# Strassen blocks in the output projection of two batches, and v through DRAM from a later pair on, in a fused attention and bilinear FFN kernel

## The chip, the cores and the metric

The kernel runs on one core of one Trainium2 chip. The metric is device time in microseconds for one execution. A core has five instruction streams: PE (TensorE, matmuls), DVE (VectorE), ACT (ScalarE), POOL (GpSimd) and SP (SyncE, here only for issuing DMAs). SBUF is the memory in which tiles lie, and PSUM (`ps` in the profile, eight banks) takes what PE writes.

## The reference

```python
# q, k, v: (4 batches, 8 heads, 768 tokens, 64), float32; sort_net: (4, 8, 8, 8)
P = sort_net
for _ in range(5):                       # exp, then rows and columns normalised
    P = exp(P - max(P)); P = P / sum(P, -1); P = P / sum(P, -2)
k_sorted = einsum('bhij,bhjcd->bhicd', P, k_blocks)   # 8 blocks of 96 tokens are mixed
v_sorted = einsum('bhij,bhjcd->bhicd', P, v_blocks)
attn = softmax(q_blocks @ k_sorted.T / 8)             # within each block of 96
x = (attn @ v_sorted).transpose(...).reshape(3072, 512)
out = ((x @ w_a) * (x @ w_b)) @ w_out                 # 512 -> 1536 -> 512
```

## The kernel before, in words

The work runs batch by batch, and attention within a batch by pairs of heads (four pairs, named (batch, pair) below).

**Attention of a pair.** q, k and v come by POOL's DMA queue. PE transposes q (line 473) and mixes k with the block weights `s_all` (L489). v goes one of two ways, chosen by `VDMA(b, p)`. By PE: v is mixed as k is (L489), cast to `vT`, transposed on PE (L559) and copied to `vs`. Through DRAM: v is mixed the other way round by two matmuls (L537), cast to `vm`, stored to a DRAM tile `vd` by SP (L546) and read back by SP into `vs` in the order wanted (L550). Then come the scores (L578), the exponentials on ACT (L583), the products with v (L593), the normalisation on DVE (L599, L604), and the transposition into `xT`, for batch 1 and later by a transposing DMA on SP (L620). There is one `xT`, so a batch's `xT` can be written only when the batch before has been read out.

**First FFN layer.** For batch 0, plain matmuls (L749) give a and b in blocks of 128 by 384. For batches 1 to 3, `ab_strassen` (matmuls at L831) works by 2 by 2 blocks with seven products for eight. For each of six groups g it runs a chain for a and one for b. Its sums of weights (`ws_a`, `ws_b`) and of x (`tx`) are made ahead. ACT copies partial results out of a bank (`f<-ps`, L840), DVE adds another bank to them (`a<-f,ps`, `f<-f,ps`), and the product of a and b goes to `hT`. Three of the four products of a group read two SBUF tiles (`hT<-a,f`) and may run on POOL or on DVE; the fourth reads a bank (`hT<-a,ps`) and runs on DVE. All these DVE and POOL operations are issued by the helper `tt`, so they share one line, L306, and are told apart by their tiles.

**Output projection.** `out_plain` makes a chunk of 128 tokens by 512 columns with twelve matmuls of 512 columns (L899), six chunks a batch; ACT or DVE copies the bank to an `o` tile and SP stores it in two DMAs (L919).

**Order.** Every piece of work is an `Op` with its engines and their assumed durations, its predecessors, and the ring buffers and banks that it takes (`get`) and gives back (`put`). `Plan.solve` is a list scheduler: of all ready pieces it takes the one that can start first, with ranks for ties, and where a piece may run on several engines, the one that it takes to end first. What comes out is a fixed order of instructions for each engine; on the chip each engine runs its own in that order and waits on semaphores. The main loop gives the ranks: output projection of batch b, attention of batch b+2, then the first layer of batch b+1.

Of the kernel before, what the change touches and what calls it, by code (L numbers as in the profile page):

```python
# [9 lines left out]
FP32 = mybir.dt.float32  # L10
# [6 lines left out]
def _ap(t: bass.AP, extra_offset, pattern):  # L17
    return bass.AP(tensor=t.tensor, offset=t.offset + extra_offset,
                   ap=[list(p) for p in pattern])
# [16 lines left out]
class Plan:  # L36
# [12 lines left out]
    def add(self, eng, dur, fn, deps=(), get=(), put=(), rank=0.0, lat=None):  # L49
        alts = dict(eng) if isinstance(eng, (list, tuple)) else {eng: dur}  # L50
        op = Op(alts, fn, deps, list(get), list(put), rank, lat, len(self.ops))
        for key in op.put:
            self.holders[key] = self.holders.get(key, 0) + 1
        self.ops.append(op)
        return op
# [76 lines left out]
    def solve(self):  # L132
        self.banks, self.until = [0.0] * 7 + [self.warm_until], {}
        for op in self.ops:
            op.left = len(op.deps)
            for d in op.deps:
                d.users.append(op)
        at = dict(self.AT)
        ready = [op for op in self.ops if op.left == 0]
        done = 0  # L140
        while ready:
            cands = {}
            for op in ready:
                w = self._when(op)
                if w is None:
                    continue
                w = max(w, op.ready)
                ends = {e: max(at[e], w) + d for e, d in op.alts.items()}
                e = min(ends, key=ends.get)
                cands.setdefault(e, []).append((max(at[e], w), op))  # L150
            pick = None
            for e, c in cands.items():
                lo = min(s for s, _ in c) + self.EPS[e]
                s, op = min(((s, o) for s, o in c if s <= lo), key=lambda x: (x[1].rank, x[1].seq))
                if pick is None or (s, op.seq) < (pick[0], pick[2].seq):
                    pick = (s, e, op)
            if pick is None:
                raise RuntimeError("the plan is stuck: " + ", ".join(
                    f"{o.get}" for o in ready[:12]))
            s, e, op = pick  # L160
            ready.remove(op)
            op.start, op.eng, op.end = s, e, s + op.alts[e]
            at[e] = op.end
            self._take(op, s)
            lat = self.LAT[e] if op.lat is None else op.lat
            self._give(op, op.end + lat)
            for u in op.users:
                u.left -= 1
                u.ready = max(u.ready, op.end + lat)
                if u.left == 0:  # L170
                    ready.append(u)
            done += 1
        assert done == len(self.ops), f"{len(self.ops) - done} pieces of work wait for ever"
        self._fill()
        return sorted(self.ops, key=lambda o: (o.start, o.seq))
# [13 lines left out]
            t = max(t, o.end)  # L189


STRASSEN_AB = (1, 2, 3)
STRASSEN_OUT = ()
QDMA = lambda b, p: b >= 3
VDMA = lambda b, p: b >= 1


@with_exitstack
def kernel(
# [11 lines left out]
    nc = tc.nc  # L211
# [34 lines left out]
    def copy(eng, out, in_):  # L246
        if eng is nc.scalar:
            nc.scalar.copy(out=out, in_=in_)  # L248
        else:
            eng.tensor_copy(out=out, in_=in_)  # L250
# [3 lines left out]
    def ring(cls, n, shape, dtype):  # L254
        mats[cls] = [const.tile(shape, dtype, name=f"{cls}{i}") for i in range(n)]
        plan.slots(cls, n)
# [3 lines left out]
    def buf(key):  # L260
        cls, i = plan.where[key]
        if cls == "pair":
            touched.update((2 * i, 2 * i + 1))
            return ps[i]
        if cls == "bank":
            touched.add(i)
            return ps[i // 2][:, i % 2, :]
        return mats[cls][i]
# [14 lines left out]
    ring("tx", 1, [P, 4, 2, HW], BF16)  # L283
    ring("a", 8, [P, HW], BF16)
    ring("f", 10, [P, HW], FP32)
    ring("o", 3, [P, DMODEL], FP32)
    w_a_sb = const.tile([P, KA, DFF], BF16, name="w_a_sb")
    w_b_sb = const.tile([P, KA, DFF], BF16, name="w_b_sb")
    w_out_sb = const.tile([P, KO, DMODEL], BF16, name="w_out_sb")
# [8 lines left out]
    rsum = const.tile([BH, NB], FP32, name="rsum")  # L298
    csum = const.tile([BH, NB], FP32, name="csum")
    p_fin = const.tile([BH, NB, NB], BF16, name="p_fin")  # L300
    p_rep = const.tile([BH, NB, NB, CG], BF16, name="p_rep")
    warm_sb = const.tile([P, 512], BF16, name="warm_sb")
    vdram = {}

    def tt(eng, out, in0, in1, op):
        ENG[eng].tensor_tensor(out=out, in0=in0, in1=in1, op=op)  # L306
# [106 lines left out]
    for it in range(5):  # L413
        last = add("ACT", 0.26, lambda: nc.scalar.activation(out=p_nat, in_=p_nat, func=AF.Exp),
                   [last], rank=-9)
        last = add("DVE", 0.21, lambda: nc.vector.reduce_sum(out=rsum, in_=p_nat, axis=AX.X),
                   [last], rank=-9)
        last = add("DVE", 0.19, lambda: nc.vector.reciprocal(out=rsum, in_=rsum), [last], rank=-9)
        last = add("DVE", 0.21, lambda: nc.vector.tensor_mul(
            out=p_nat, in0=p_nat, in1=_ap(rsum, 0, [[NB, BH], [1, NB], [0, NB]])), [last], rank=-9)  # L420
        last = add("DVE", 0.26, lambda: nc.vector.reduce_sum(
            out=csum, in_=p_nat.transpose([0, 2, 1]), axis=AX.X), [last], rank=-9)
        last = add("DVE", 0.19, lambda: nc.vector.reciprocal(out=csum, in_=csum), [last], rank=-9)
        last = add("DVE", 0.21, lambda it=it: nc.vector.tensor_mul(
            out=p_fin if it == 4 else p_nat, in0=p_nat,
            in1=_ap(csum, 0, [[NB, BH], [0, NB], [1, NB]])), [last], rank=-9)
    reps = [add(e, d, lambda h=h, e=e: copy(
        ENG[e], p_rep[:, h * NBH:(h + 1) * NBH],
        _ap(p_fin, h * NBH * NB, [[NB * NB, BH], [NB, NBH], [1, NB], [0, CG]])), [last], rank=-9)
        for h, e, d in ((0, "DVE", 0.42), (1, "ACT", 0.62))]  # L430

    def spread_ops(h):
        t = buf("pc")[:, 0:NB * BH].rearrange("p (j h) -> p j h", j=NB)
        for i in range(NB):
            nc.tensor.matmul(t[:, i, :], lhsT=p_rep[:, i], rhs=ident[0:BH, 0:BH],
                             start=True, stop=True)
    o_pc = add("PE", 0.36, lambda: spread_ops(0), reps + [o_ident], get=[("bank", "pc")], rank=-9)

    def spread(eng, src, h0, n):
        eng.tensor_tensor(  # L440
# [369 lines left out]
    def ab_strassen(b, g, rk, ws_ok, tx_ok, hdeps):  # L810
# [3 lines left out]
        def chain(n, w_sb, ws):  # L814
            kA, kX, kY = ("A", b, g, n), ("X", b, g, n), ("Y", b, g, n)

            def w(half, kk, j):
                return w_sb[:, 2 * kk + j, (half * G + g) * P:(half * G + g + 1) * P]
# [4 lines left out]
            def xb(kk, t, j):  # L823
                return buf(("xT", b))[:, 2 * kk + j, t * HW:(t + 1) * HW]
# [10 lines left out]
            def pe(key, lf, rf, start, stop, deps, r, get=(), put=()):  # L835
                return add("PE", 0.325, lambda: mm(key, lf, rf, start, stop), deps, get=get,
                           put=put, rank=r)
# [6 lines left out]
            def plus(name, key, deps, put, r):  # L844
# [5 lines left out]

            wd = [w_in[n, c], w_in[n, c + 2]]
            r = rk + (0.02 if n == "b" else 0.0)
            p1 = pe(kA, lambda j, w=w: w(0, 0, j), lambda j: xb(0, 0, j), True, False, x + wd, r,
                    get=[("chain", ("ch", b, g, n)), ("bank", kA)], put=[("xT", b)])
            s1 = snap("s1", p1, r)
            p2 = pe(kX, lambda j, w=w: w(0, 1, j), lambda j: xb(1, 0, j), True, True, x + wd, r + 0.1,
                    get=[("bank", kX)], put=[("xT", b)])
            c11 = plus("s1", kX, [s1, p2], [kX, ("s1", b, g, n)], r)("c11")
            p6 = pe(kA, lambda j, s=s: s(1, j), lambda j: tb(1, j), False, False,
# [33 lines left out]
    def out_plain(b, t, c, rk, last=False):  # L893
# [28 lines left out]
                    in_=o_sb[u * NBH * CG:(u + 1) * NBH * CG])  # L922
        sp_dma(1.2, 0.8, store, [op], put=[("o", b, t, c)], rank=rk)


    plan.slots("chain", 4)
    for p in range(HP):
        rk = float(p)
        qd = q_part(0, p, 0, rk)
        kd = mix_half(0, p, "k", 0, rk)  # L930
        vd = v_part(0, p, 0, mix_half(0, p, "v", 0, rk + 0.05), rk + 0.1)
        m = so_part(0, p, 0, True, kd, qd, vd, rk + 0.1)
        x_part(0, p, 0, m, rk + 0.15)
        st["last", p] = m
# [23 lines left out]
    for p in range(HP):  # L958
        attention(1, p, R1 + 6.0 * p)
    ws_ok = w_sums(R0 + 30.0)  # L960
    RB = R0 + 60.0
    for b in range(B):
        for t in range(2):
            for c in range(3):
                out_plain(b, t, c, RB + 40.0)
        if b + 1 == B:
            break
        if b + 2 < B:
            for p in range(HP):
                attention(b + 2, p, RB + 36.0 + 0.5 * p)  # L970
            if b + 3 < B:
                for p in range(HP):
                    load_pair(b + 3, p, 40 + p, st["last", b + 2, 3])
        tx_ok = x_sums(b + 1, RB + 49.0)
        for g in range(G):
            ab_strassen(b + 1, g, RB + 50.0 + 4 * g, ws_ok, tx_ok, out_last[b])
        RB += 100.0

# [84 lines left out]
```

## Time and profile before

| | |
|---|---|
| median of 11 runs | 251.98 us (251.23 to 255.49) |
| profiled execution, its time and its span | 252.46 us, 250.7 us |
| PE, DVE, ACT, POOL busy | 95%, 62%, 49%, 46% |
| L899 matmuls (projection), 128x512 | x276 in the records, 64.1 us |
| POOL hT<-a,f, DVE hT<-a,f | x34 at 919 ns, x20 at 580 ns |
| DVE a<-f,ps and f<-f,ps | x54 and x54 at 548 and 547 ns |
| vd<-vm, vs<-vd (SP's queue) | x12 and x12, 2.7 and 3.1 us to landing |

A row of the profile names line, engine, operation and tiles as out<-in, with the count, the busy time and the mean of one. Matmul durations there include the time in the pipeline, so a matmul's pace is read from the distance between starts. The wait column names what ended an engine's idle time. Line numbers are those of the kernel before.

### The profile page before, as it was taken

Reading aid. Unit: us, or ns where it says so; the run is one execution under the profiler, and the core shown is the slowest. Engines: PE = TensorE matmul, PEld = TensorE weight load, DVE = VectorE, ACT = ScalarE, POOL = GpSimd, SP = SyncE. Lnnn points to the kernel's source line nnn. Section 1 sums busy time; section 2 is a strip of 40 time slices with the busy share of each in tenths; the row PEclk is TensorE's granted clock in tenths of the full one; section 3 lists DMA queues with packets and bytes.
Section 4 is the critical chain, followed back from the end, with each engine's and each line's share of the span. In section 5 each row is a group of like instructions: output and inputs, shape, how many; then the busy total and the mean of one; then the engine's idle time right before and its main releaser. Section 6 shows DMA issues by size and latency. Waiting matters only on the chain.

```text
span 250.7 us, 5624 instructions
## 1 busy us (share of the span) xinstructions
PE 236.9 (95%) x2153; PEld 132.6 (53%) x2168; DVE 154.5 (62%) x355; ACT 122.9 (49%) x239; POOL 114.9 (46%) x127
## 2 busy tenths in 40 slices
PE   7898999997699999999999999999999999999992
PEld 2466666654366445556554445555554455565440
DVE  6656645554348546688889463789886149787120
ACT  3267455455065621576754363867741156664110
POOL 8879999999950002019955100036250004445000
PEclk9999799999799999999999999999999999999998
DMA  5999999999972985525999966500034550000135
GB/s 70 175 202 163 203 201 182 165 189 221 167 125 63 160 196 101 140 72 70 153 135 148 154 165 176 141 3 0 0 65 78 121 115 3 1 0 0 44 84 126
DMA packets 51962, 28.68 MB, mean 114 GB/s; under 512 B 30432, under 2 KB 48864, under 8 KB 51936
## 3 DMA queue, kind: packets, MB, share of 16 engines
q0 software_dynamic: 24112, 14.16, 42.2%
q1 hardware_dynamic: 27824, 14.17, 26.8%
q8 instruction: 17, 0.28, 0.5%
q14 instruction: 9, 0.07, 0.1%
HBM read 30.68 MB, written 8.65 MB: 157 GB/s over the span
## 4 chain that ended last, share of the span: by engine, by line
PE 89%; DMA 5%; POOL 2%; issue 1%; ACT 1%; DVE 0%
PE ps L831 33%; PE ps L899 25%; PE ps L749 13%; PE ps L593 4%; PE ps L578 3%; DMA q<-in_q_dram 3%; DMA vs<-vd 2%; PE ps L500 2%; PE ps L473 2%; PE ps L489 2%; PE ps L537 2%; PE ps L983 1%; PE ps L559 1%; PE ps L612 1%; ACT eT L583 1%
## 5 line engine op out<-in xcount | busy, mean ns | idle before, releaser
L306 POOL TENSOR_TENSOR hT<-a,f 128x384 bf16<-128x384 bf16 x34 | 31.1, 919 | 81.9 <-DVE f L306 80.8
L899 PE MATMUL ps<-w_out_sb,hT 128*128 128x512 bf16 x276 | 64.1, 379 | 0.7 <-issue 0.2
L840 ACT COPY f<-ps 128x384 f32<-128x384 f32 x108 | 48.3, 481 | 22.7 <-PE ps L831 18.4
L899 PEld LDWEIGHTS <-hT 128*128 128x128 bf16 x288 | 27.0, 98 | 30.5
L306 DVE TENSOR_TENSOR f<-f,ps 128x384 f32<-128x384 f32 x54 | 29.0, 547 | 6.4 <-PE ps L831 5.0
L306 DVE TENSOR_TENSOR a<-f,ps 128x384 bf16<-128x384 f32 x54 | 29.5, 548 | 5.7 <-PE ps L831 4.2
L306 DVE TENSOR_TENSOR hT<-a,ps 128x384 bf16<-128x384 bf16 x42 | 23.1, 549 | 14.8 <-PE ps L749 8.0
L583 ACT ACTIVATE eT<-ps 96x768 bf16<-96x768 f32 x32 | 25.5, 807 | 11.0 <-PE ps L578 10.6
L248 ACT COPY o<-ps 128x512 f32<-128x512 f32 x14 | 8.1, 585 | 34.7 <-PE ps L899 31.6
L831 PE MATMUL ps<-tx,ws_b 128*128 128x384 bf16 x108 | 25.0, 326 | 0.0
L831 PE MATMUL ps<-tx,ws_a 128*128 128x384 bf16 x108 | 24.8, 327 | 0.0
L755 ACT CAST a<-ps 128x384 bf16<-128x384 f32 x24 | 11.5, 479 | 21.1 <-PE ps L749 17.6
L604 DVE TENSOR_TENSOR xp<-ps,rec 96x512 bf16<-96x512 f32 x32 | 21.4, 680 | 0.4
L250 DVE COPY o<-ps 128x512 f32<-128x512 f32 x10 | 6.9, 689 | 22.5 <-PE ps L899 22.5
L749 PE MATMUL ps<-xT,w_a_sb 128*128 128x384 bf16 x96 | 20.5, 339 | 0.0
L749 PE MATMUL ps<-xT,w_b_sb 128*128 128x384 bf16 x96 | 20.2, 335 | 0.0
L831 PEld LDWEIGHTS <-ws_a 128*128 128x128 bf16 x144 | 13.4, 98 | 10.3 <-ACT f L840 1.6
L248 ACT CAST kT<-ps 128x768 bf16<-128x768 f32 (+1 forms) x17 | 11.9, 706 | 13.8 <-PE ps L489 12.2
L831 PEld LDWEIGHTS <-ws_b 128*128 128x128 bf16 x144 | 13.4, 98 | 9.7 <-ACT f L840 1.1
L250 DVE CAST vm<-ps 128x768 bf16<-128x768 f32 x12 | 11.5, 955 | 11.2 <-PE ps L537 6.2
L831 PE MATMUL ps<-xT,w_b_sb 128*128 128x384 bf16 x72 | 17.5, 326 | 0.1
L831 PE MATMUL ps<-xT,w_a_sb 128*128 128x384 bf16 x72 | 17.5, 326 | 0.0
(88 smaller groups left out, 338.3 us busy)
## 6 DMA issues: line engine op xcount, KB each, us to landing
out_dram<-o SPq DMA_DIRECT2D x48, 128.0 KB, 2.4
k<-in_k_dram POOLq DMA_DIRECT2D x16, 192.0 KB, 6.3
v<-in_v_dram POOLq DMA_DIRECT2D x16, 192.0 KB, 6.8
vd<-vm SPq DMA_DIRECT2D x12, 192.0 KB, 2.7
vs<-vd SPq DMA_DIRECT2D x12, 192.0 KB, 3.1
q<-in_q_dram POOLq DMA_DIRECT2D x16, 96.0 KB, 7.1
w_a_sb<-in_moe_w_a_dram POOLq DMA_DIRECT2D x4, 384.0 KB, 7.8
w_b_sb<-in_moe_w_b_dram POOLq DMA_DIRECT2D x4, 384.0 KB, 8.3
```

The lines of the kernel that those rows point to most:

```text
L248: nc.scalar.copy(out=out, in_=in_)
L250: eng.tensor_copy(out=out, in_=in_)
L306: ENG[eng].tensor_tensor(out=out, in0=in0, in1=in1, op=op)
L578: nc.tensor.matmul(sc[:, e, i * BLK:(i + 1) * BLK], lhsT=kT[e * D:(e + 1) * D, at:at + P], rhs=rhs, start=True, stop=True)
L583: nc.scalar.activation(out=buf(("eT", b, p, h))[:, :, 0:HB], in_=buf(("sc", b, p, h))[0:BLK, :, 0:HB], func=AF.Exp, scale=float(scale))
L593: nc.tensor.matmul(ops_[:, e, i * OW:(i + 1) * OW], lhsT=eT[:, e, i * BLK:i * BLK + P], rhs=vs[:, h * NBH + i, e * OW:(e + 1) * OW], start ...
L604: nc.vector.tensor_tensor(out=_ap(xp, h * NBH * 2 * D, [[NB * 2 * D, BLK], [D, 2], [2 * D, NBH], [1, D]]), in0=_ap(ops_, 2, [[1024, BLK], ...
L749: nc.tensor.matmul(pf[:, 0:HW], lhsT=w_sb[:, kc, m * P:(m + 1) * P], rhs=buf(("xT", b))[:, kc, t * HW:(t + 1) * HW], start=(kc == 0), stop ...
L755: ea = add("ACT", 0.48, lambda: nc.scalar.copy(out=buf(("a", b, t, m)), in_=buf(("pf", b, t, m, "a"))[:, 0:HW]), [pa], get=[("a", ("a", b, ...
L831: nc.tensor.matmul(buf(key)[:, 0:HW], lhsT=lf(j), rhs=rf(j), start=start and j == 0, stop=j == 1, skip_group_check=not start)
L840: return add("ACT", 0.48, lambda: nc.scalar.copy(out=buf((name, b, g, n)), in_=buf(kA)[:, 0:HW]), [dep], get=[("f", (name, b, g, n))], rank=r)
L899: nc.tensor.matmul(po, lhsT=hT[:, t * 2 + m // G, m % G, c * P:(c + 1) * P], rhs=w_out_sb[:, m, :], start=(m == 0), stop=(m == KO - 1), sk ...
```

## The change

The output projection of batches 2 and 3 is made by `out_strassen` in place of `out_plain`. It takes three chunks a batch, each of 2 by 128 tokens (one chunk of each token half t), with four 128 by 256 results and seven products of six matmuls of 256 columns (L1007 of the changed kernel). Sums of blocks of `w_out` (eight of 128 by 768, made once, in free `q2` and `kT` buffers) and of `hT` (24 of 128 by 384 for each batch, in free `k2` and `v2` buffers) are made in bf16 ahead of it, on DVE or POOL. ACT snaps and DVE sums put the results together, as in `ab_strassen`. Results of the second token half go to four buffers cut out of `s_all` (`os`). The first product of batch 3's first layer gets a dependence on the last p5 of batch 2's projection.

Pairs (1,0) and (1,1) get v by PE; the DRAM way begins at pair (1,2). The `o` ring has four buffers for three, and `p_rep` loses its own tile and lies in one of them at the start. In the scheduler, a piece that may run on several engines and isn't the pick of the engine on which it would end first is now offered to its other engines as well.

```diff
 # Plan.solve
-            cands = {}
+            cands, open_ = {}, []
...
                 cands.setdefault(e, []).append((max(at[e], w), op))
+                if len(ends) > 1:
+                    open_.append((w, op, e))
...
+            picks = {e: best(e) for e in cands}
+            for w, op, e in open_:
+                if picks[e][1] is not op:
+                    for e2 in op.alts:
+                        if e2 != e:
+                            cands.setdefault(e2, []).append((max(at[e2], w), op))
...
-STRASSEN_OUT = ()
+STRASSEN_OUT = (2, 3)
-VDMA = lambda b, p: b >= 1
+VDMA = lambda b, p: 4 * b + p >= 6
...
-    ring("o", 3, [P, DMODEL], FP32)
+    ring("o", 4, [P, DMODEL], FP32)
...
 # ab_strassen
-            p1 = pe(kA, ..., True, False, x + wd, r,
+            p1 = pe(kA, ..., True, False, x + wd + [st.get(("lasty", b - 1))], r,
...
+    def o_sums(rank):                      # sums of blocks of w_out
...
+                op = add((("DVE", 0.55), ("POOL", 1.75)), None, None,
+                         wo_in + [st["last", B - 1, HP - 1]] + [ok[i, u] for i in need],
+                         get=[("q2" if n < 6 else "kT", ("wt", j, u))], rank=rank)
...
+    def out_strassen(b, rk, wt_ok):
...
+        for g in range(G):                 # sums of blocks of hT: S0 to S3 for each g
...
+            todo = ((0, lambda g=g: (hb(1, 0, g), hb(1, 1, g)), ALU.add, h21 + h22, None),
+                    (1, lambda g=g: (sb(0, g), hb(0, 0, g)), ALU.subtract, h11, 0),
+                    (2, lambda g=g: (hb(0, 0, g), hb(1, 0, g)), ALU.subtract, h11 + h21, None),
+                    (3, lambda g=g: (hb(0, 1, g), sb(1, g)), ALU.subtract, h12, 1))
+            for j, src, alu, deps, need in todo:
+                op = add((("DVE", 0.33), ("POOL", 0.92)), None, None, ...
...
+            p1 = pe(kA, h(0, 0), wo(0, 0), True, True, hd(0, 0, first) + wo_in, rk, ...
+            s1 = snap("os1", p1)
+            p2 = pe(kX, h(0, 1), wo(1, 0), True, True, hd(0, 1, first) + wo_in, rk + 0.1, ...
+            c11 = plus("os1", kX, 0, 0, [s1, p2], [kX, ("os1", b, c)])
+            p6 = pe(kA, s(1), wt(1), False, True, [s1] + sd(1) + td(1), rk, put=sput(1) + tput(1))
+            u2 = snap("ou2", p6)
+            p5 = pe(kY, s(0), wt(0), True, True, sd(0) + td(0), rk + 0.1, ...
+            st["lasty", b] = p5
+            p7 = pe(kA, s(2), wt(2), False, True, [u2] + sd(2) + td(2), rk, put=sput(2) + tput(2))
+            u3 = snap("ou3", p7)
+            p4 = pe(kZ, h(1, 1), wt(3), True, True, [p1, p2] + hd(1, 1) + td(3), rk + 0.6, ...
+            c22 = plus("ou3", kY, 1, 1, [u3, p5], [("ou3", b, c)])
+            c21 = plus("ou3", kZ, 1, 0, [u3, p4], [kZ, ("ou3", b, c), ("och", b, c)])
+            p3 = pe(kY, s(3), wo(1, 1), False, True, [c22] + sd(3), rk, put=sput(3))
+            c12 = plus("ou2", kY, 0, 1, [u2, p3], [kY, ("ou2", b, c), ("och", b, c)])
...
+            sp_dma(1.2, 0.8, lambda store=store: store(0), [c11, c12], put=[("o", b, 0, c)], rank=rk)
+            sp_dma(1.2, 0.8, lambda store=store: store(1), [c22, c21], put=[("o", b, 1, c)], rank=rk)
...
+        if b in STRASSEN_OUT:
+            if wt_ok is None:
+                wt_ok = o_sums(RB - 10.0)
+            out_strassen(b, RB + 40.0, wt_ok)
+        else:
+            for t in range(2):
+                for c in range(3):
+                    out_plain(b, t, c, RB + 40.0)
```

## The prediction

> **What bounds the kernel now.** I read the page first: busy shares, then the chain of work that ended last.
>
> ```profile
> PE 236.9 (95%) x2153; PEld 132.6 (53%) x2168; DVE 154.5 (62%) x355; ACT 122.9 (49%) x239; POOL 114.9 (46%) x127
> ...
> PE 89%; DMA 5%; POOL 2%; issue 1%; ACT 1%; DVE 0%
> PE ps L831 33%; PE ps L899 25%; PE ps L749 13%; PE ps L593 4%; PE ps L578 3%; DMA q<-in_q_dram 3%; DMA vs<-vd 2%; PE ps L500 2%; PE ps L473 2%; PE ps L489 2%; PE ps L537 2%; PE ps L983 1%; PE ps L559 1%; PE ps L612 1%; ACT eT L583 1%
> ```
>
> PE is the bound: 89% of the chain is matmuls, a quarter of it L899, the output projection. The one other thing on the chain that the change touches is the DMA vs<-vd. The answer on waits shows it as a single wait, and PE's timeline shows what it costs:
>
> ```profile
> PE ps L593 <- DMA vs<-vd: 4.2, 1, 4.2
> ```
>
> ```profile
> 60.02 0.81 PE L749 MATMUL ps<-xT,w_a_sb 128*128 128x384 bf16 x4
> 65.04 1.04 PE L593 MATMUL ps<-vs,eT 96*128 96x66 bf16 x16 [4.20 <-DMA vs<-vd]
> 65.89 1.47 PE L749 MATMUL ps<-xT,w_b_sb 128*128 128x384 bf16 x4
> 67.15 1.33 PE L749 MATMUL ps<-xT,w_a_sb 128*128 128x384 bf16 x4
> ```
>
> Besides the 4.2 idle, the chain gives the 16 L593 after it 1.04 us (0.5 to 0.6 elsewhere) and the 8 L749 2.41 (1.30 elsewhere): the wait costs 4.2 + 0.4 + 1.1 = 5.7 us.
>
> Next the windows by stage (us, PE, PEld, DVE, ACT, POOL): batch 2's L831 stage with the rest of batch 3's attention, L899 of batch 2, batch 3's L831 stage.
>
> ```profile
> 157.00:189.30 32.30, 32.10 (x235) 18.58 (x234) 26.97 (x58) 21.69 (x46) 11.91 (x13) 1.00 0.17 38
> 189.30:202.60 13.30, 13.25 (x62) 6.03 (x62) 4.19 (x9) 1.86 (x4) 0.00 (x0) 1.00 0.50 109
> 202.60:230.00 27.40, 27.35 (x168) 16.18 (x168) 22.43 (x45) 18.77 (x43) 10.42 (x12) 1.00 0.09 20
> ```
>
> PE never waits there, but DVE is 82 to 84% busy, POOL 37 to 38%. So DVE has about 5 us to spare per stage, and POOL is the free one. Last, two lines of the timeline near 136 us:
>
> ```profile
> 134.55 1.84 POOL L306 TENSOR_TENSOR hT<-a,f 128x384 bf16<-128x384 bf16 x2 [1.31 <-DVE f L306]
> ...
> 135.89 0.91 DVE L306 TENSOR_TENSOR hT<-a,f 128x384 bf16<-128x384 bf16 x1
> ```
>
> This DVE product reads two SBUF tiles. Usually it takes 0.55 to 0.56; here POOL was at work until 136.39, and it ended at 136.80, 0.41 after POOL. The two others of 30 such DVE operations that met POOL also ended 0.41 after it (one took 0.69). The 108 DVE sums that read one operand from ps (a<-f,ps and f<-f,ps) average 0.55 whether POOL runs or not.
>
> [...] 62 L899 of 512 columns in 13.4 us are 0.216 each, 8 L749 of 384 in 1.30 are 0.1625. [...]
>
> **The change part by part.** Instructions are counted in the order in which the changed kernel has them on each engine.
>
> *v.* Pairs (1,0) and (1,1) get v by PE. Each swaps 2 L537 (0.33 to 0.43) for 12 L489 (0.34 to 0.46), +0.05, and adds 8 L559 at 0.33 per four, +0.65: +1.4 for both. Casts move among DVE and ACT, which have room there; SP and the DMA engines lose two trips. The 5.7 us wait goes. What is late next is the third pair's trip. From its L537 to its L593 stand 36 L749, 32 L578 and the fourth pair's start: 5.85 + 0.9 + 1.2 = 7.95 us. Its trip is a cast with its start (1.2), vd (3.5 landing at 70.7 us), and vs (2.6 at 74.3; 3.9 at 65.5): 7.3 to 9 us. I take a 0.5 us wait (ends 0 and 5.7, a repeat of today's). The fourth vs stands behind three xT transposes on SP, as it does now. Sum: -5.7 + 1.4 + 0.5 = **-3.8**.
>
> *PE of batches 2 and 3.* 72 matmuls of 512 columns become 126 of 256. No row has 256 columns; [...] 0.109 each (estimate). 72 x 0.216 = 15.5 against 13.8: 1.77 per batch, **-3.5**. If weight loads (98 ns mean) showed through at 0.118, 2.3 less gain[...].
>
> *Batch 2's L831 stage.* The eight w_out sums (768 wide, 1.65 on POOL as ws_a) all go to POOL as soon as batch 3's attention is done, with four hT products between them: 8 x 1.65 + 4 x 0.92 = 16.9 us without a pause. POOL then has no room for hT, so DVE has 13 of its 18 hT<-a,f, against 5. From there to the stage's end PE has 146 x 0.1625 + 33 x 0.109 = 27.3 us; DVE has 38 with an operand in ps x 0.548, 13 x 0.557 and one sum at 0.35: 28.4 us. DVE already fills the stage. Each of the 13 also meets the lock. An operation that arrives at a random point of a POOL one of length L waits (L - 0.14)^2 / 2L on average: 0.69 for 1.65, 0.33 for 0.92. About eight meet the w_out sums at 0.6, the other five a half-busy POOL: 4.9 + 0.8 = 5.7. Queued behind a blocked DVE operation are the ps sums that free the banks; PE waits for those. PE can run about one chain ahead, so I take **+4.5** (ends 0.6, no lock, and 7).
>
> *Start of batch 2's projection.* Its second sum S1 needs the last hT. After the last L831, PE has 3 + 12 ready matmuls and five of the next six (2.2 us). DVE does sum, sum, product and five sums at about 0.3 (half of tx's 0.548, up to 0.35): 2.9 to 3.3 us. Without the lock PE waits 0.7 to 1. With POOL doing its S sums (about 0.9) at the same time, the two take turns, and four DVE sums at 1.1 put it at 6.8, a wait of 4.6. I take **+2.0**.
>
> *Batch 3's L831 stage.* DVE: 36 + 6 at 0.548, 7 at 0.557, 3 sums: 28 us in a 29 us window. POOL is about 75% busy (11 hT, 13 sums): 10 x 0.75 x 0.33 = 2.5, less the 1 us of room and some lead of PE: **+1.0** (0 to 3). The new dependence on the last p5 costs nothing: PE's order has it earlier anyway.
>
> *Start of batch 3's projection.* 25 ready matmuls (2.7 us) and five more cover the last sums without the lock; three or four turns at 0.6 use that up: **+0.8** (0 to 2.5). Inside both projections six-matmul groups of 0.65 alternate over three chunks, as long as a snap plus a DVE sum (0.38 + 0.42, from 0.48 and 0.55 at 384): nothing. ACT loses copies of 0.59 and gains snaps; it is 14% busy there.
>
> *End.* Today one copy (0.59) and two DMA issues (0.57 each) follow the last matmul. In the new order five stores, ten issues, end the SP queue, the first ready 2.2 us before PE ends: the last issue starts 2.9 us after PE, against 1.1: **+1.9** (1.0 to 2.2). Buffers o and os (four each) never fill; p_rep's move is nothing: o gets its first result after L899 starts at 82 us.
>
> Sum: -3.8 - 3.5 + 4.5 + 2.0 + 1.0 + 0.8 + 1.9 = **+2.9 us**, on the profiled execution's 252.46: 255.4. That execution lies 0.5 above the median, so 254.9.
>
> **Rivals.**
> *DVE keeps pace.* If hT products rarely meet POOL, or PE's lead covers it, the lock costs 0 and the values without the lock hold: -3.8 - 3.5 + 0.6 + 0.8 + 0 + 0.3 + 1.9 = -3.7, 248.3. For it: before, only 3 of 30 met POOL. Against it: POOL was 37% busy and DVE had 5 us spare. It decides if the lock costs under some 3.7 us in all.
> *The third pair waits as the first did* (on top of the forecast): +5.2, near 260. For it: POOL's loads still run until 70 us. Against it: trips that start after 65 us take 3.5 to 3.9, not 6, and two trips are gone.
> *Weight loads bound the 256-column matmuls:* +2.3, 257.2. Against it: weight loads at 98 ns lie under 109, and 16 L593 with a load each run in 0.51.
> That the change doesn't do what it says is excluded: the new order has 252 matmuls of 256 columns and 20 L537 for 24.
>
> **How the numbers follow.** 0.5%, 1.3 us, is about what a measurement of this kernel can tell from no change. Forecast 0.60 (0.54 slower, 0.06 within), DVE keeps pace 0.25 (0.22 faster, 0.03 within), third pair waits 0.10 and weight loads 0.05 (slower). So faster 0.22, within 0.09, slower 0.69. Both signs hold weight. The forecast's own range, with its ends not all at once, is 251.5 to 260; down to the first rival with about one in ten outside on each side: 248.0 to 260.0.
>
> **What would show it.** In the changed profile: no vs<-vd wait over 1 us near 60 us; the 256-column row at 0.109 from start to start; hT<-a,f on DVE with a mean near 1 us and single ones up to 2; PE waits on DVE between 160 and 195; PE's end 6.8 us before the span's. PE without gaps in batch 2's L831 stage would make the forecast wrong; a gain with DVE at 1 us a product would too.

## The result, and the profile after

The changed kernel takes 255.37 us (median of 12 runs, 254.14 to 256.15) against 252.46 for the kernel before (47 runs in all): the ratio is 1.0143, 95% interval 1.0119 to 1.0167, so it is slower by 1.4%. The total was forecast at 254.9. Three terms of its sum were wrong by 2.6 to 5.2 us each, not all in the same direction, and the experiments below are mostly about these. What the forecast calls the lock is what it read near 136 us: a DVE product of two SBUF tiles ended 0.41 us after POOL had ended. The profiled execution took 255.77 us, with a span of 254.0. Every experiment was timed beside runs of the kernel before on the same chip. Ratios leave disturbed runs out, so a ratio isn't always the quotient of the two medians given; differences in us are between medians, and those of the kernel before were 252.46 to 252.65 in all rounds.

First the page of the changed kernel: busy shares, and the chain that ended last by engine and by line.

```profile
PE 234.3 (92%) x2300; PEld 142.6 (56%) x2312; DVE 180.3 (71%) x399; ACT 125.4 (49%) x251; POOL 154.9 (61%) x159
...
PE 76%; DVE 12%; DMA 5%; issue 3%; POOL 1%; ACT 1%; SPq 0%; DVEq 0%
PE ps L845 27%; PE ps L763 12%; PE ps L914 10%; PE ps L1007 9%; DVE hT L316 6%; PE ps L607 3%; DMA vs<-vd 3%; PE ps L592 3%; PE ps L1148 2%; DVE f L316 2%; PE ps L487 2%; PE ps L503 2%; PE ps L514 2%; DMA q<-in_q_dram 2%; DVE v L316 1%
```

PE is busy for 2.6 us less than before, DVE for 26 and POOL for 40 more. DVE had no part in the chain before; now it holds 12% of it, half of that in hT products. What PE waits for (total, number, longest):

```profile
PE ps L1007 <- DVE v L316: 5.4, 2, 4.1
...
PE ps L607 <- DMA vs<-vd: 0.9, 1, 0.9
PE ps L514 <- issue: 0.7, 2, 0.5
PE ps L1007 <- DVE hT L316: 0.7, 1, 0.7
```

The 4.2 us wait for vs has become one of 0.9, at the third pair. In its place stands a 4.1 us wait of the new projection (L1007) for a sum of hT blocks, which lies in a free `v2` buffer and so is called v. The windows show where this is (us, PE, PEld, DVE, ACT, POOL, granted clock, DMA): batch 2's L845 stage (L831 before), the start and rest of batch 2's projection, batch 3's L845 stage.

```profile
150.00:185.20 35.20, 33.38 (x248) 20.19 (x247) 34.44 (x64) 20.43 (x45) 27.58 (x22) 1.00 0.12 25
185.20:203.60 18.40, 13.53 (x97) 10.06 (x96) 13.21 (x26) 3.16 (x9) 9.90 (x9) 0.81 0.20 42
203.60:232.40 28.80, 28.73 (x180) 16.90 (x178) 26.00 (x50) 18.17 (x42) 21.30 (x23) 1.00 0.19 44
```

In the first window DVE is busy for 34.44 of 35.20 us, and PE waits for it for 1.9 us in all:

```profile
PE ps L1007 <- DVE f L316: 1.0, 1, 1.0
PE ps L845 <- DVE f L316: 0.7, 1, 0.7
PE ps L845 <- DVE a L316: 0.2, 1, 0.2
```

In the second, PE is idle for nearly 5 of 18.4 us, and its clock is 0.81. The timeline around 190 us, PE first, then DVE and POOL (start, length, count; in brackets the idle time before):

```profile
186.99 1.49 PE L1007 MATMUL ps<-kT,hT 128*128 128x256 bf16 x12 [0.68 <-DVE hT L316]
192.56 0.80 PE L1007 MATMUL ps<-q,k 128*128 128x256 bf16 x3 [4.09 <-DVE v L316]
193.15 0.85 PE L1007 MATMUL ps<-q,v 128*128 128x256 bf16 x3
193.79 0.85 PE L1007 MATMUL ps<-q,k 128*128 128x256 bf16 x3
...
197.54 0.49 PE L1007 MATMUL ps<-q,k 128*128 128x256 bf16 x3
197.87 0.38 PE L1007 MATMUL ps<-q,v 128*128 128x256 bf16 x2
```

```profile
185.07 1.86 DVE L316 TENSOR_TENSOR hT<-a,f 128x384 bf16<-128x384 bf16 x2
...
187.84 1.26 DVE L316 TENSOR_TENSOR hT<-a,f 128x384 bf16<-128x384 bf16 x1
189.02 3.02 DVE L316 TENSOR_TENSOR v<-hT 128x384 bf16<-128x384 bf16 x3
191.96 0.34 DVE L316 TENSOR_TENSOR v<-v,hT 128x384 bf16<-128x384 bf16 x1
192.23 0.61 DVE L316 TENSOR_TENSOR k<-hT,k 128x384 bf16<-128x384 bf16 x2
```

```profile
186.48 2.21 POOL L316 TENSOR_TENSOR k<-hT 128x384 bf16<-128x384 bf16 x2
188.64 1.22 POOL L316 TENSOR_TENSOR v<-hT 128x384 bf16<-128x384 bf16 x1
189.82 1.02 POOL L316 TENSOR_TENSOR k<-hT,k 128x384 bf16<-128x384 bf16 x1
190.81 1.02 POOL L316 TENSOR_TENSOR v<-hT,v 128x384 bf16<-128x384 bf16 x1
```

Read the three together. From 187.8 to 191.8 POOL makes its last sums while DVE makes the last hT product and three sums, about one us for each. As soon as POOL is done, at 191.83, DVE's sums take 0.3 each. PE starts again at 192.56, and its groups of three now start 0.64 apart; from 197.5 on 0.33, which is 0.109 a matmul. The trace gives the granted clock as one half from 190.6 to 197.4. In the first 2.0 of these 6.8 us PE is still waiting and loses nothing by it; in the 4.8 us from 192.56 on it does half the work. So the half clock costs 2.4 us on top of the wait. (The eight groups from 192.56 to 197.54 take 4.98 us; at full clock they would take 2.6.)

The step at the end is also visible. PE's last matmul starts at 246.75, and SP's queue issues ten DMAs after the results have come, the last six from the buffers in s_all:

```profile
244.89 2.38 SPq L1070 DMA_DIRECT2D out_dram<-o  x4
247.37 3.75 SPq L1070 DMA_DIRECT2D out_dram<-s_all  x6
```

From the start of the last matmul to the end of the span are 7.2 us, against 5.3 before (245.39 to 250.66).

### The profile page after: what moved, and what is told of

Its sections match the earlier page's. It is cut to its first block, busy times and chain, and to the rows that moved or that the text cites. A ratio compares the mean times of both kernels' runs of the same rounds, so it can differ in the third digit from the quotient of the medians.

```text
span 254.0 us, 6022 instructions
## 1 busy us (share of the span) xinstructions
PE 234.3 (92%) x2300; PEld 142.6 (56%) x2312; DVE 180.3 (71%) x399; ACT 125.4 (49%) x251; POOL 154.9 (61%) x159
## 4 chain that ended last, share of the span: by engine, by line
PE 76%; DVE 12%; DMA 5%; issue 3%; POOL 1%; ACT 1%; SPq 0%; DVEq 0%
PE ps L845 27%; PE ps L763 12%; PE ps L914 10%; PE ps L1007 9%; DVE hT L316 6%; PE ps L607 3%; DMA vs<-vd 3%; PE ps L592 3%; PE ps L1148 2%; DVE f L316 2%; PE ps L487 2%; PE ps L503 2%; PE ps L514 2%; DMA q<-in_q_dram 2%; DVE v L316 1%
## 5 line engine op out<-in xcount | busy, mean ns | idle before, releaser
L316 POOL TENSOR_TENSOR hT<-a,f 128x384 bf16<-128x384 bf16 x25 | 23.1, 929 | 48.0 <-DVE f L316 33.9
L597 ACT ACTIVATE eT<-ps 96x768 bf16<-96x768 f32 x32 | 24.8, 806 | 21.6 <-PE ps L592 19.5
L914 PE MATMUL ps<-w_out_sb,hT 128*128 128x512 bf16 x135 | 32.8, 379 | 0.8 <-issue 0.5
L316 DVE TENSOR_TENSOR hT<-a,f 128x384 bf16<-128x384 bf16 x29 | 25.1, 880 | 0.2
L845 PE MATMUL ps<-tx,ws_b 128*128 128x384 bf16 x108 | 25.1, 326 | 0.0
L845 PE MATMUL ps<-tx,ws_a 128*128 128x384 bf16 x108 | 24.6, 327 | 0.0
L914 PEld LDWEIGHTS <-hT 128*128 128x128 bf16 x144 | 13.0, 98 | 13.9
L763 PE MATMUL ps<-xT,w_a_sb 128*128 128x384 bf16 x96 | 19.6, 327 | 0.0
L763 PE MATMUL ps<-xT,w_b_sb 128*128 128x384 bf16 x96 | 19.6, 326 | 0.0
L845 PEld LDWEIGHTS <-ws_a 128*128 128x128 bf16 x144 | 13.2, 98 | 10.8 <-ACT f L854 1.4
L1028 ACT COPY f<-ps 128x256 f32<-128x256 f32 x18 | 6.4, 374 | 24.9 <-PE ps L1007 24.9
L845 PEld LDWEIGHTS <-ws_b 128*128 128x128 bf16 x144 | 13.4, 98 | 9.1 <-ACT f L854 0.5
L845 PE MATMUL ps<-xT,w_b_sb 128*128 128x384 bf16 x72 | 17.4, 326 | 0.7 <-DVE f L316 0.7
L845 PE MATMUL ps<-xT,w_a_sb 128*128 128x384 bf16 x72 | 17.3, 326 | 0.0
L1007 PE MATMUL ps<-q,k 128*128 128x256 bf16 x54 | 10.2, 305 | 5.4 <-DVE v L316 5.4
L845 PEld LDWEIGHTS <-w_b_sb 128*128 128x128 bf16 x108 | 10.1, 98 | 8.7 <-ACT f L854 1.2
```

The source lines that it names most:

```text
L597: nc.scalar.activation(out=buf(("eT", b, p, h))[:, :, 0:HB], in_=buf(("sc", b, p, h))[0:BLK, :, 0:HB], func=AF.Exp, scale=float(scale))
L763: nc.tensor.matmul(pf[:, 0:HW], lhsT=w_sb[:, kc, m * P:(m + 1) * P], rhs=buf(("xT", b))[:, kc, t * HW:(t + 1) * HW], start=(kc == 0), stop ...
L845: nc.tensor.matmul(buf(key)[:, 0:HW], lhsT=lf(j), rhs=rf(j), start=start and j == 0, stop=j == 1, skip_group_check=not start)
L914: nc.tensor.matmul(po, lhsT=hT[:, t * 2 + m // G, m % G, c * P:(c + 1) * P], rhs=w_out_sb[:, m, :], start=(m == 0), stop=(m == KO - 1), sk ...
L1007: nc.tensor.matmul(buf(key)[:, 0:HD], lhsT=lf(g), rhs=rf(g), start=start and g == 0, stop=stop and g == G - 1, skip_group_check=True)
L1028: return add("ACT", 0.37, lambda: nc.scalar.copy(out=buf((name, b, c))[:, 0:HD], in_=buf(kA)[:, 0:HD]), [dep], get=[("f", (name, b, c))], ...
```

## The experiments

**One part at a time.** Four kernels were run together: the changed kernel without Strassen in the projection, without the v part, without the w_out sums, and without either main part.

```diff
 # v_only                          # strassen_only
-STRASSEN_OUT = (2, 3)             -VDMA = lambda b, p: 4 * b + p >= 6
+STRASSEN_OUT = ()                 +VDMA = lambda b, p: b >= 1
 # rest_only: both of these edits
 # no_w_sums: p4 to p7 take blocks of w_out itself, o_sums isn't called
-            return lambda g: buf(("wt", j, g // 3))[...]
+            return wo(j % 2, j // 2)
```

Expected of v_only: 

> The changed kernel with the output projection of all batches plain: of the change, the v part, the scheduler rule and the buffers are left. All theories: the 5.7 us wait of the first pair goes, 1.4 us of PE work comes, so 4 us under before, 248.5 (ratio 0.984). The rival that the third pair's trip waits as the first did: 252 (ratio 1.00). If the changed kernel's lead at 74 us was only an early start of that one profiled execution: 252.

Expected of strassen_only: 

> The changed kernel with v through DRAM from the first pair of batch 1 on, as before. If the two parts add up: 255.4 + 4 = 259.4 (ratio 1.027), with the wait for vs<-vd near 60 us back. If they interact (the Strassen loss being smaller when batch 2 comes later): 256 to 257.

Expected of no_w_sums: 

> The changed kernel without the eight sums of blocks of w_out: the products p4, p5, p6 and p7 take blocks of w_out itself, so this part of the computation is left out. PE has the same 252 matmuls of 256 columns, the sums of hT stay. POOL has 13 us less to do and takes 32 of the hT<-a,f products, DVE 22 instead of 29. Theory of POOL and DVE (load and lock): batch 2's L845 stage loses its 3 us of waits and the projection starts with less, 250 to 252. Theory that the projection's own chain of snaps and sums costs the time: unchanged, 255.

Expected of rest_only: 

> The changed kernel with both options as before: only the scheduler rule, four o buffers and p_rep's place are left. Expected within 1 us of before, 251.5 to 253.5, the vs<-vd wait still there. Rival: the scheduler rule alone moves products from POOL to DVE and costs 1 to 2 us.

| kernel | median us (range) | ratio to before, 95% interval |
|---|---|---|
| v_only | 244.49 (243.82 to 244.56) | 0.9673 (0.9636 to 0.9709) |
| strassen_only | 263.89 (263.44 to 264.35) | 1.0447 (1.0406 to 1.0488) |
| no_w_sums | 246.67 (246.13 to 246.92) | 0.9762 (0.9726 to 0.9799) |
| rest_only | 254.51 (251.62 to 256.88) | 1.0107 (1.0042 to 1.0172) |

The v part is worth 8 us and Strassen costs 11; each is far more than the sum had it (-3.8 and +6.7), and the two errors nearly cancel. Of the 11, 8.7 go when the w_out sums go (255.37 to 246.67). Plain projections with the new v, v_only, beat both kernels. Rest_only isn't below the kernel before: with the old way for v the scheduler's rule and the fourth o buffer bring nothing. (All these kernels keep one more small part of the change: in `ab_strassen` the second product of a chain now depends on the first.)

None of the four came out in the range expected of it. v_only gained twice what was expected. strassen_only's profile has a wait for vs of 6.3 us, longer than the 4.2 of the kernel before. no_w_sums gained 3.3 us more than the better end of its range. And rest_only was slower by 1.1%, as its rival had it, but its profile has only one hT product more on DVE (21 for 20), so the rival's reason isn't shown; three of its four runs lie between 251.62 and 254.70.

**v alone, and for all of batch 1.** v_alone is the kernel before with the one line changed; v_batch1 is v_only with pairs (1,2) and (1,3) by PE as well.

```diff
 # v_alone (on the kernel before)  # v_batch1 (on v_only)
-VDMA = lambda b, p: b >= 1        -VDMA = lambda b, p: 4 * b + p >= 6
+VDMA = lambda b, p: 4*b + p >= 6  +VDMA = lambda b, p: 4 * b + p >= 8
```

> The kernel before with VDMA = 4 * b + p >= 6 and nothing else. By the prediction's sum for v (-3.8) it takes 248.6. Clock theory: the wait for the first vs also halves PE's clock for one window (3.4 us lost) in nearly every run of the kernel before (its mean granted clock is 0.983 to 0.986 in all of them), and the sum took only 1.5 of it; then v alone is worth about -6 to -8.5, 244 to 246.5, with a mean clock of 0.995 or more and no wait of PE for vs over 1 us. If the gain needs the scheduler's rule or the fourth o buffer (with which the v part was measured so far), it stays above 248.

v_alone took 244.94 us (244.69 to 245.98) against 252.64 on that chip: 0.9715, 0.9637 to 0.9794. The line for vs in its list of waits of PE:

```profile
PE ps L593 <- DMA vs<-vd: 0.5, 1, 0.5
```

So the v part needs none of the other edits. Its mean granted clock was 0.996 to 1.0 in every run, and that of the kernel before in the same rounds 0.973 to 0.993, with 0.985 in the middle. The profiled executions say what that is worth: the kernel before has two half-clock stretches of 3.4 us (what the expectation calls a window), from 27.2 to 30.6 and from 64.8 to 68.2 us, in which PE lost 1.7 and 1.6 us (in the second it was waiting until 65.04), and v_alone, whose mean in its profiled execution is 1.0, has none. So some 3 of the 7.7 us are clock. The clock theory's numbers held, but its reason only in part: only the second stretch follows the wait for vs, and it costs 1.6 us and not 3.4.

> The changed kernel with the plain output projection in all batches, and all of batch 1's v by PE (VDMA = 4 * b + p >= 8). Against the version that keeps pairs (1,2) and (1,3) through DRAM (244.49): by the price of the swap in the prediction, 0.7 us of PE for each pair, +1.4, less whatever PE still waits for the third pair's vs (none over 0.2 in that profile), so 245.2 to 246.0. Rival: the trips of the third and fourth pair still cost through SP's queue and the DMA engines, 243.5 to 244.2.

v_batch1 took 244.73 us (ratio 0.9683, 0.9605 to 0.9762), which can't be told from v_only's 244.49. PE's busy time is 234.2 us, against 232.9 in v_only, whose record lacks 16 matmuls, and 233.8 in v_alone. So between 0.4 and 1.3 us of the 1.4 priced for two pairs show in PE's work, and hardly any reaches the time. Neither theory's range held.

**The disputed operations by themselves.**

> Computes nothing of the reference (its output is zeros); it only issues the disputed DVE and POOL operations, in phases with a barrier between them. Alone: DVE product hT<-a,f 0.55 us, POOL sum of 128x768 bf16 1.65, DVE sum of 128x384 bf16 0.30 to 0.35, POOL the same sum 0.92. Lock theory (a DVE operation with two SBUF inputs and a POOL operation exclude each other for a whole instruction): with eight 128x768 POOL sums beside twelve DVE products, the two take turns, so each DVE product takes 1.65 to 2.1 until POOL is done; with a DVE product that reads one operand from ps, 0.55 as alone; ten POOL sums beside twelve DVE sums of 128x384: each DVE sum 0.9 to 1.3. Load theory (no lock, DVE simply has more to do in the changed kernel): all DVE durations as alone. The last phase, POOL memsets (which only write) beside DVE products, tells whether a write alone excludes: 0.55 if not.

DVE's timeline in that kernel (products alone, beside 768-column sums of POOL, with one operand from ps, then sums alone, beside sums, and products beside memsets), and POOL's:

```profile
3.72 3.84 DVE L59 TENSOR_TENSOR hT<-a,f 128x384 bf16<-128x384 bf16 x8 [0.82 <-ACT a L55]
19.86 16.89 DVE L59 TENSOR_TENSOR hT<-a,f 128x384 bf16<-128x384 bf16 x12 [12.31 <-ACT a L55]
38.53 5.66 DVE L63 TENSOR_TENSOR hT<-a,ps 128x384 bf16<-128x384 bf16 x12 [1.78 <-ACT a L55]
52.24 2.24 DVE L67 TENSOR_TENSOR wsum<-a,b 128x384 bf16<-128x384 bf16 x8 [8.05 <-ACT a L55]
64.17 10.12 DVE L67 TENSOR_TENSOR wsum<-a,b 128x384 bf16<-128x384 bf16 x12 [9.69 <-ACT a L55]
76.07 6.11 DVE L59 TENSOR_TENSOR hT<-a,f 128x384 bf16<-128x384 bf16 x12 [1.78 <-ACT a L55]
```

```profile
8.97 9.58 POOL L71 TENSOR_TENSOR ws<-w,w 128x768 bf16<-128x768 bf16 x6 [8.53 <-ACT w L54]
19.50 14.96 POOL L71 TENSOR_TENSOR ws<-w,w 128x768 bf16<-128x768 bf16 x8 [0.94 <-ACT w L54]
38.16 12.77 POOL L71 TENSOR_TENSOR ws<-w,w 128x768 bf16<-128x768 bf16 x8 [3.70 <-ACT w L54]
```

The times here are from start to start (a single product is listed with about 0.55). Alone a product takes 3.84/8 = 0.48 us and a sum 0.28. With the second operand in ps a product beside POOL's sums takes no longer: 5.66/12 = 0.47, and POOL's eight take 1.60 each as alone. With both operands in SBUF the two engines alternate here: while POOL works, each DVE product takes as long as a POOL sum, 14.96/8 = 1.87, and each DVE sum of 0.28 beside POOL's sums nearly one us (12 in 10.12). The memsets on POOL held no product up: in the last phase the first product met a POOL sum that was still running and took 0.96, the other eleven took (6.11 - 0.96)/11 = 0.47 each. The lock theory's numbers held. What on the chip causes this was not shown; the lock below stands for what was measured: beside sums of POOL, a DVE product with two SBUF operands waits for a whole instruction of POOL (1.87), and beside memsets it doesn't (0.47).

**Which lock it is.** Memsets can thus stand in for POOL's work without the lock (0.47 us a product beside them). Three kernels keep the changed kernel's order on every engine and replace POOL's w_out sums, POOL's share of the 24 sums of hT blocks that each batch needs (S sums for short), or both.

```diff
 # pool_fill, in o_sums            # s_fill, in out_strassen's S sums
-   tt(op.eng, tb(j, u), ...)      -   tt(op.eng, sb(j, g), ...)
+   if op.eng == "POOL":           +   if op.eng == "POOL":
+       for n in (768, 768, 320):  +       for n in (384, 384, 64):
+           nc.gpsimd.memset(...)  +           nc.gpsimd.memset(...)
 # both_fill: both
```

> The changed kernel in the same order on every engine, but each of the eight POOL sums of w_out blocks is replaced by three POOL memsets of its tile (768, 768 and 320 columns, 1.65 us together by the 0.68 us that one of 768 took alone), which only write and did not hold up a DVE product when measured by themselves. It leaves out the w_out sums, so the projections of batches 2 and 3 use zeros in p4 to p7. POOL stays as occupied, and DVE keeps its 29 hT<-a,f. Lock theory: DVE's products in batch 2's L845 stage fall back toward 0.55, PE's waits there and most of the 4.1 us wait at the start of batch 2's projection go, and with it the halved clock: 248 (247 to 250), near the 246.67 of the kernel without the sums. Load theory (what costs is that POOL is occupied, so that DVE has 29 instead of 22 hT products): 254 to 255.5.

pool_fill took 254.37 us (ratio 1.0073, 1.0043 to 1.0104), only 1.0 us less than the changed kernel. DVE's operations that write or read hT, in two windows (us, busy time, count, clock), first in pool_fill, then at the same places in the changed kernel:

```profile
157.00:176.00 19.00, 6.27 (x12) 1.00 0.00 1
183.00:192.00 9.00, 7.92 (x12) 0.89 0.24 45
```

```profile
157.00:176.00 19.00, 9.11 (x11) 1.00 0.00 1
184.60:193.60 9.00, 7.92 (x12) 0.83 0.23 45
```

In the first window, beside the memsets, they take 0.52 each and not 0.83, so the lock of the w_out sums is gone; in the second, beside the S sums, 12 of them (products and sums) take 7.92, exactly as in the changed kernel, and PE's wait of 4.1 us and the halved clock are still there. This was a miss of the lock theory as it was put: by what they lock, the w_out sums cost only 1.0. (p4 to p7 multiply by zeros here, and the mean clock of the second window is still 0.89.)

> The changed kernel in the same order on every engine, its w_out sums left as they are, but every S sum of hT blocks that POOL makes is replaced by three POOL memsets (384, 384 and 64 columns, about 0.92 us together). It leaves out POOL's S sums, so p3 and p5 to p7 of batches 2 and 3 use zeros there. Theory of the last sums: what costs is DVE and POOL in turns at the end of batch 2's L845 stage (DVE's last three hT<-a,f at 1.26 and 0.9, three v<-hT in 3.02, POOL's sums at 1.0 to 1.2), because POOL's S sums start only when the w_out sums are done; then the 4.1 us wait at the start of batch 2's projection shrinks to under 1.5, the clock stays whole, and the time is 249 (248 to 250.5). Theory of the backlog alone (POOL's S sums come too late in its own order, whoever holds the lock): the wait stays over 3 us and the time is 253.5 to 255.5.

s_fill took 247.76 us (247.42 to 248.58; ratio 0.9862, 0.9772 to 0.9951), 7.6 less than the changed kernel, with all eight w_out sums still on POOL. The same stretch of DVE's timeline as above, and PE's:

```profile
183.13 1.02 DVE L316 TENSOR_TENSOR hT<-a,f 128x384 bf16<-128x384 bf16 x2
...
184.79 0.56 DVE L316 TENSOR_TENSOR hT<-a,f 128x384 bf16<-128x384 bf16 x1
185.26 0.89 DVE L316 TENSOR_TENSOR v<-hT 128x384 bf16<-128x384 bf16 x3
```

```profile
184.20 1.48 PE L1012 MATMUL ps<-kT,hT 128*128 128x256 bf16 x12
186.68 0.49 PE L1012 MATMUL ps<-q,k 128*128 128x256 bf16 x3 [1.00 <-POOL k L985]
```

The three sums take 0.89 for 3.02, PE waits 1.0 for 4.1, and the clock stays whole (1.00 from 183 to 192 us, 0.997 in the mean of the execution), all as the theory of the last sums had it; the time lies just under its range. POOL isn't earlier or quicker for it: its memsets run from 175.7 to 191.3 us without a pause, where its sums ran from 176.2 to 191.8. So what is gone is only what they held up on DVE.

> The two replacements together: POOL's w_out sums and POOL's S sums are memsets of the same length, the order is that of the changed kernel. It leaves out both kinds of POOL sums. What remains against the kernel without w_out sums (246.67) is DVE's seven more hT<-a,f and POOL's occupied time; what it gains over the run with POOL's S sums alone replaced is the lock of the w_out sums, 1.0 us by the run that replaced only them (255.37 to 254.37). Theory of the last sums: 248 (247 to 249.5). Theory of the backlog alone: 252.5 to 254.5.

both_fill took 247.41 us (246.45 to 249.59; ratio 0.9849, 0.9759 to 0.9939), no different from s_fill. What is left above no_w_sums, 0.7 us, lies within the spread of its four runs, so the seven more hT products on DVE cost little as long as nothing holds them up.

**Half of the w_out sums early.** If the S sums are what hurts, and the w_out sums cost by pushing them to the end of the stage, a shorter queue on POOL should be enough. half_early makes four w_out sums early, in vT buffers.

```diff
-    wo_in + [st["last", B - 1, HP - 1]] + ...
-    get=[("q2" if n < 6 else "kT", ("wt", j, u))]
+    wo_in + [st["last", 1, 1] if j in (0, 2) else st["last", B - 1, HP - 1]] + ...
+    get=[("vT" if j in (0, 2) else "q2", ("wt", j, u))]
```

> The changed kernel with four of the eight w_out sums (j = 0 and 2) made early, in the four vT buffers, which are free once pair (1,1) is done; the planner gives them to DVE around batch 1's first layer. The other four stay after batch 3's attention on POOL. The result is the reference's. Lock theory: half the POOL sums that DVE meets in batch 2's L845 stage go, and POOL reaches the S sums some 6 us earlier, so at least half of the 8.7 us that the w_out sums cost in all: 250.5 (249 to 252), with the clock at 1.0 at the start of batch 2's projection. Load theory: DVE keeps 29 or more hT<-a,f and gets four more sums, 255 or more.

It took 250.09 us (249.86 to 250.19; ratio 0.9892, 0.9863 to 0.9922), 5.3 less than the changed kernel, though DVE has 31 hT<-a,f and their mean is still 848 ns. Its windows for batch 2's stage and projection:

```profile
152.70:185.30 32.60, 32.51 (x238) 19.84 (x237) 31.76 (x61) 20.25 (x45) 25.72 (x25) 1.00 0.13 27
185.30:197.80 12.50, 10.08 (x86) 7.74 (x86) 9.72 (x18) 3.16 (x9) 5.12 (x6) 1.00 0.26 53
```

The projection's window is 12.5 us for 18.4 (with 86 matmuls for 97), at full clock. The stage starts 2.7 us later (152.7 for 150.0). The early sums didn't run around batch 1's first layer, as I had written, but at once, from 62.7 to 71.2 us in batch 0's plain stage, where POOL was at work too: they took 1.73 us each, and PE waited 2.6 us for DVE there. So this remedy gives part of its gain back. How late POOL comes to its S sums goes with the gain: in the changed kernel it begins them at 176.2 us, in half_early at 163.3, in no_w_sums at 161.5.

**The clock by itself.** keep_warm puts 34 matmuls with a zero operand ahead of the 4.1 us wait.

```diff
+            if b == 2 and c == 0:      # 34 x 256 columns, added to bank kA as zeros
+                fill = [add("PE", 0.0, zeros, [s1], rank=rk)]
-            p6 = pe(kA, s(1), wt(1), False, True, [s1] + sd(1) + td(1), ...
+            p6 = pe(kA, s(1), wt(1), False, True, [s1] + fill + sd(1) + td(1), ...
```

> The changed kernel with 34 matmuls of 256 columns with a zero operand (they add zeros to a bank) put on PE just ahead of the wait at the start of batch 2's projection; order otherwise the same, the result too. Clock theory: the 4.1 us wait for the hT sums halves the clock for 6.8 us (190.6 to 197.4), which costs 3.4 us on top of the wait; with PE kept busy the clock stays at 1.0 and the time is 252.0 (251.5 to 253). If the clock isn't what PE loses there (DVE behind it sets the pace anyway), 255 to 255.5.

It took 253.71 us (20 runs, 252.48 to 255.37; ratio 1.0043, 1.0020 to 1.0066), so 1.7 us less. PE's timeline there:

```profile
188.07 3.88 PE L1056 MATMUL ps<-warm_sb 128*128 128x256 bf16 x34
191.78 0.82 PE L1007 MATMUL ps<-kT,hT 128*128 128x256 bf16 x6
192.84 0.49 PE L1007 MATMUL ps<-q,k 128*128 128x256 bf16 x3 [0.24 <-issue]
193.16 0.49 PE L1007 MATMUL ps<-q,v 128*128 128x256 bf16 x3
```

The groups of three start 0.33 apart at once, for 0.64 in the changed kernel. From the end of batch 2's L845 stage to the start of batch 3's are 15.9 us, for 18.4: 2.4 us came back there, as much as the half clock cost by the count above; the 3.4 expected had also counted the half clock in which PE was still waiting. The median lies above the range expected, and only 1.7 under the changed kernel's, while single runs spread over 2.9 us; where the remaining 0.7 stays, the run doesn't show.

## Why the prediction was right, and where it was wrong

The sign, the total and most of the named signs were right: no wait for vs over 1 us near 60, the 256-column matmuls at 0.109 (where the line through the measured 0.1625 of 384 columns and 0.216 of 512 puts them), a mean of 880 ns for hT<-a,f on DVE and waits of PE on DVE between 160 and 195. But that the total came within half a microsecond is luck: three of its terms were off by more than that, and the errors nearly cancelled. The profile puts each step where it belongs.

| step | predicted us | measured us, and where |
|---|---|---|
| v | -3.8 | -7.7 (v_alone); -8.5 (strassen_only to the changed kernel) |
| PE of projections | -3.5 | pace 0.109 as assumed, so as predicted |
| batch 2's L831 stage | +4.5 | 1.9: PE's waits on DVE from 150 to 185 us (1.0 + 0.7 + 0.2) |
| start of batch 2's projection | +2.0 | 7.2: 4.8 of waits (0.7 + 4.1) and 2.4 of half clock |
| batch 3, stage and start | +1.8 | from its first L845 to its last L1007 43.1 us, to 42.8 before; +0.4, less its PE gain of 1.8: +2.2 |
| end | +1.9 | +1.9 (7.2 for 5.3) |

With -7.7 for v the measured column makes +2.0, and the medians differ by 2.9; the 0.9 between them isn't placed.

**The v term was mis-sized.** The waits and the clock after the first were right: 4.2 us of wait, 1.5 of slow matmuls behind it (1.6 by the times of the clock), and the third pair's wait (0.5 predicted, 0.9 in the changed kernel, 0.5 in v_alone). Two other things were not. The 1.4 of added PE work seems to lie in time that PE had. And the execution shown has the other half-clock stretch, at 27.2 to 30.6 us, which I didn't count; it cost 1.7. The mean clocks say that nearly every run of the kernel before loses about as much in all as the profiled one, and v_alone hardly any. But this stretch lies over 30 us ahead of the wait for vs, and up to it PE has the same matmuls in the same order in both kernels, so the wait for vs can't have caused it; why v_alone's runs are spared stays open. -4.2, -1.5, -1.7 and +0.5 make -6.9 of the -7.7.

**The start of batch 2's projection was mis-sized.** I had worked out what happens, "the two take turns, and four DVE sums at 1.1 put it at 6.8, a wait of 4.6", as the upper end, and took the middle. The runs show that it is what happens when DVE has several two-SBUF operations in a row beside sums of POOL: each product took 1.87 us in lock_bench, for 0.48 alone, and the three sums here 3.02, for 0.89 in s_fill. The formula for a random arrival fits single products (the six on DVE between 160 and 176 us took 1.06 us on average, 0.5 over the 0.55 alone, where I had taken 0.6), not this. And I gave a wait of 4 us no clock, though I had counted 1.5 us of slow matmuls after the vs wait of the same length: 2.4 us more. Two waits ended at half clock: the 4.1 us of the changed kernel (half from 190.6 to 197.4) and the 4.2 of the kernel before (half from 64.8 to 68.2). How long PE must wait for that was not shown. And no such wait stands ahead of the stretch at 27.2 us in the kernel before: in the 3.4 us ahead of it PE was busy for 2.9.

**The lock was put in the wrong place.** The +4.5 in the stage was for hT products that meet w_out sums. Freed of that lock, the kernel gained 1.0 us (pool_fill). The w_out sums cost 8.7 all the same, because they stand ahead of the S sums on POOL: these run at the end of the stage, where DVE has its last products and sums to make and PE has nothing else ready. Freeing the S sums alone gave 7.6. In the stage itself PE waited 1.9 us and not 4.5: 33 first matmuls of the projection, which were ready, were done inside it. That the rest of DVE's lag came out when these were used up is how I read it; no run shows that by itself.

**The rivals.** DVE didn't keep pace, the third pair waited 0.9 us and not as the first had, and weight loads didn't bound the 256-column matmuls (0.109 from start to start; the 0.118 put for that case was the author's estimate). The condition put for the first rival, a lock under 3.7 us in all, was the right question: it costs about 8 with the clock (255.37 to 247.41 in both_fill).

## What to carry to other kernels

Price a wait of PE like the two of 4.1 and 4.2 us here with the clock that it takes afterwards, and count for that only the time in which PE works: of 6.8 us at half clock 4.8 counted here, which is 2.4 us. Look for half-clock stretches elsewhere too, and at the mean granted clock of all runs, not only at the profiled one: the stretch at 27.2 us, of which the forecast took no account, was worth 1.7. When work goes to POOL, ask what stands behind it in POOL's queue and whether that will run beside DVE operations with two SBUF operands on the path of PE; there take the alternating price, a POOL instruction for each DVE one (1.87 us for 0.48 in lock_bench). Saving 3.5 us of PE work was no gain here, because the operands for it had to be made by DVE and POOL in a stage that DVE already filled; plain projections with the new v (244.49 us) beat it by 10.9 us, and beat even no_w_sums (246.67), which leaves a part of that work out.

## What was not expected of the hardware

While DVE and POOL alternated in lock_bench, POOL paid as well: its 768-column sum took 1.87 us for 1.60. A POOL memset of the same 768 columns took 0.68 us from start to start, and the DVE products beside the memsets 0.47.

The trace of the kernel before has two half-clock stretches of 3.41 us, with 34.13 at full clock between them, and that of the changed kernel one of 6.83; what sets these lengths was not shown. Two waits of nearly the same length cost differently. In the kernel before the clock fell 0.3 us before the end of its wait of 4.2 us and stayed low for 3.1 us of work; in the changed kernel it fell 2.0 us before the end of its wait of 4.1 and stayed low for 4.8 us of work. Wait and clock together cost 5.8 and 6.5 us.
